# A conversion's first ScalarE step is moved from the end of one loop iteration to the middle of the next

## The chip, the cores and the metric

The kernel runs on one NeuronCore of a Trainium2 chip. The time is the device time of one execution in microseconds (us), and the number quoted is the median of several executions. The traces come from one further execution that the hardware profiler recorded. Matrix work is done by TensorE (PE in the rows, with its weight loads as PEld), elementwise work by VectorE (DVE), ScalarE (ACT) and GpSimd (POOL). All transfers are issued by SyncE (SP).

## The reference

Three layers follow each other. The first is a recurrent attention with a decaying state; the second a soft mixture of experts; the third a two-layer network with a squared ReLU. Inputs are float32.

```
for t in range(S):                                   # S = 768, 4 batches, 8 heads, D = 48
    cur = einsum('bhd,bhe->bhde', u * k_t, v_t)
    y_t = einsum('bhd,bhde->bhe', r_t, state + cur)
    state = w_t * state + einsum('bhd,bhe->bhde', k_t, v_t)
logits = x @ phi                                     # x: 3072 x 384, 32 slots
slot_in = softmax_over_tokens(logits).T @ x
slot_out[e] = relu(slot_in[e] @ w1[e]) @ w2[e]       # 8 experts, 384 -> 1024 -> 384
x = softmax_over_slots(logits) @ slot_out
h = relu(x @ w_in); out = (h * h) @ w_out            # 384 -> 2048 -> 384
```

The two weight matrices of the last layer arrive as 64-bit words. They are turned into float32 by integer arithmetic on the chip; this is what "conversion" means below.

## The kernel before

The attention runs in a loop of 33 iterations (line 531) with an order written out by hand: each engine executes its instructions in the order in which the Python code issues them. One unit is a pair of heads of one batch and half of the sequence (three chunks of 128 tokens). Iteration i works on several units at once. It starts the loads of unit i+4 and the v of unit i+2, scans the decay of unit i+2 (`scan0`, `scan1`, on DVE), transposes k of unit i+1 (`ktr`, on PE), and forms the state of unit i and the output of unit i-1. Batch b fills iterations 8b to 8b+7, and while the next batch runs, `slot` places its logits, softmax and slot sums into four places of the iterations.

The ring that passes through every iteration is this. `kvmm` (PE, tile psacc) multiplies the transposed k, `Kn`, with v. `state` (DVE, lines 252 and 254, tile S) adds the result to the decayed state. `tmul` (ACT, line 265, tile Tb) scales S, four small activations in even iterations and six in odd ones. `ycopy` (ACT, line 280) takes the output of the unit before from PSUM. `pend` (line 191) takes the decay products. `kcopy` (ACT, line 233) takes the transposed k from PSUM into `Kn`, and with that the next `kvmm` can begin. ACT's order in an iteration is tmul, ycopy, pend, kcopy, a small copy `dc` (line 174), and the copies of `slot`. DVE's order is scan0, state, a reciprocal, kprod, scan1, `amask` (line 218), two conversion steps, and the reductions of `slot`. GpSimd's is `diag0` (line 166, it needs a loaded rk), `diag5` (line 178), `rprod` (line 207, it needs scan1's F) and the last conversion step.

In 16 of the iterations a piece of w_in, 128 x 384 words, is converted. `LDW` is the list of iterations at whose end a piece j is loaded (5, 6, 7, 9, 10, 11, 13, 14, 15, 17, 18, 19, 21, 22, 23, 25). Line 465 issues this load into one of two buffers in turn. `wconv` (line 409) returns the four steps of a conversion:

```
q0: cc.q  = low words * 2^-29       ACT,  line 416
c2: cc.m  = high words << 3, masked DVE,  line 426
c3: cc.m |= sign and top bit        DVE,  line 430
c4: win   = cc.m + cc.q             POOL, line 434
```

There is one scratch tile `cc` in the loop. q0 of one conversion therefore has to wait for c4 of the conversion before it, which reads both halves of `cc`. c4 waits for its own q0 and c3. The load of piece j+2 has to wait for q0 and c3 of piece j, which read its buffer. In SP's queue the loads of the next iteration (lines 154 and 162) stand behind that load.

The list `cv` holds the steps of the conversion whose piece was loaded one iteration ago. It is filled at the end of iteration i; there q0 is issued, behind everything that iteration i gave to ACT and ahead of tmul of iteration i+1. The three other steps are issued in iteration i+1, behind `slot(i, 1)` (line 593).

Of the kernel before, what the change touches and what calls it, by code (L numbers as in the profile page):

```python
# [60 lines left out]
def rwkv_softmoe_relu2(ctx: ExitStack, tc: tile.TileContext, lt, lp, ub, vp, r, k, v, w, u, phi, phn, w1, w2, w_in, w_out, consts, xd, out):  # L61
# [72 lines left out]
    def mt(name):  # L134
        return psM.tile([128, 512], F32, tag="m", name=name)

    def warm(mt, n, src=cst[:, 0:256].bitcast(BF16)):
        ps = mt("warm")
        for _ in range(n):
            mm(ps, src[:, 0:128], src)  # L140
# [4 lines left out]
    def load(i, between=lambda: None):  # L145
        u_, hf = divmod(i, 2)
        b, p = divmod(u_, NP)
        t = {"i": i, "h": hf, "p": p, "b": b, "rk2": rk[i % NL], "w": lb[i % NW]}
        for o, c, n in ((t["w"], slice(LW, LN), NW), (t["rk2"], slice(0, LW), NL)):
            if i < n:  # L150
                nc.sync.dma_start(out=o, in_=lp[i, :, c])
            else:
                for h in range(2):
                    nc.sync.dma_start(out=o[64 * h:64 * h + D], in_=lt[b, 2 * p + h, hf, :, c])
            between()
            between = lambda: None
        t["r"], t["k"] = t["rk2"][:, 0:HT], t["rk2"][:, LK:LK + HT]
        return t

    def load_v(t):  # L160
        t["v"] = vt[t["i"] % NV]
        nc.sync.dma_start(out=t["v"][:, 0:2 * HC * D], in_=vp[t["b"], t["p"], t["h"]])
# [5 lines left out]
    def diag1(t, ps):  # L168
        for n in range(HC):
            mm(ps[:, HT + 2 * n:HT + 2 * n + 2], t["rk"][:, n * C:(n + 1) * C], uB[:, t["p"], 0:2])  # L170

    def diag2(t, ps):
        t["dc"] = P.tile([128, HC, 2], F32, tag="dc", name="dc", bufs=2)
        nc.scalar.copy(out=t["dc"], in_=chunks(ps[:, HT:HT + 2 * HC], 2))
# [7 lines left out]
    def scan0(t):  # L182
        q = t["Q"] = pq
        nc.vector.tensor_tensor_scan(
            out=q[:, 0:NZ][:, ::-1], data0=t["w"][:, ::-1], data1=b1[:, ::-1],
            initial=0.0, op0=ALU.mult, op1=ALU.add)
# [22 lines left out]
    def amm(t):  # L209
        ps = t["pA"] = psA.tile([128, 2, 512], F32, tag="A", name="psA")  # L210
        for n in range(HC):
            for h in range(2):
                q = slice(64 * h, 64 * h + 64)
                s = slice(n * C, (n + 1) * C)
                mm(ps[:, h, s], t["k"][q, s], t["r"][q, s])

    def amask(t):
        nc.vector.copy_predicated(  # L218
            out=t["A"], mask=mask.unsqueeze(1).unsqueeze(1).to_broadcast([128, HC, 2, C]),
            data=t["pA"][:, :, 0:HT].rearrange("p h (n c) -> p n h c", c=C))  # L220

    def ktr(t, t2=None):
        n = HC if t["h"] == 0 else HC - 1
        ps = t["pK"] = mt("psK")
        for j in range(n):
            tr(ps[:, j * C:(j + 1) * C], t["k"][:, j * C:(j + 1) * C])
        if t2:
            diag1(t2, ps)

    def kcopy(t, t2=None):  # L230
        n = HC if t["h"] == 0 else HC - 1
        kn = t["Kn"] = P.tile([128, HC, C], F32, tag="Kn", name="Kn", bufs=2)
        nc.scalar.copy(out=kn[:, 0:n, :], in_=chunks(t["pK"][:, 0:n * C]))  # L233
        if t2:
            diag2(t2, t["pK"])
# [4 lines left out]
    def kvmm(t):  # L240
        for n in range(HC if t["h"] == 0 else HC - 1):
            for h in range(2):
                q = slice(64 * h, 64 * h + 64)
                mm(kvs(t, n)[q], t["Kn"][:, n, q], t["v"][:, (2 * n + h) * D:(2 * n + h + 1) * D])

    def state(t, n):
        if n >= (HC if t["h"] == 0 else HC - 1):
            return
        s, kv = t["S"], kvs(t, n)
        o = t["Sn"][:, 0] if n == HC - 1 else s[:, n + 1]  # L250
        if n < (1 if t["h"] == 0 else 0):
            nc.vector.tensor_copy(out=o, in_=kv)  # L252
        else:
            nc.vector.scalar_tensor_tensor(
                out=o, in0=s[:, n], scalar=t["P"][:, n:n + 1], in1=kv, op0=ALU.mult, op1=ALU.add)

    def tmul(t, late=False):
        for n in range(1 if t["h"] == 0 else 0, HC):
            for h in range(2):
                q = slice(64 * h, 64 * h + 64)  # L260
                o, x, c = t["T"][q, n, 64 * h:64 * h + D], t["S"][q, n], t["P"][q, n:n + 1]
                if late:
                    nc.vector.tensor_scalar(out=o, in0=x, scalar1=c, scalar2=None, op0=ALU.mult)
                else:
                    nc.scalar.activation(out=o, in_=x, func=AF.Copy, scale=c)  # L265

    def ymm(t):
        ps = mt("psY")
        f = 1 if t["h"] == 0 else 0
        for n in range(HC):  # L270
            for h in range(2):
                mm(ps[64 * h:64 * h + 64, n * C:(n + 1) * C], t["v"][:, (2 * n + h) * D:(2 * n + h) * D + 64], t["A"][:, n, h, :],
                   start=(n == 0), stop=(n < f))
        for n in range(f, HC):
            s = slice(n * C, (n + 1) * C)
            mm(ps[:, s], t["T"][:, n, :], t["r"][:, s], start=False)
        t["pY"] = ps

    def ycopy(t):
        nc.scalar.copy(out=t["x"][:, t["h"] * HT:(t["h"] + 1) * HT], in_=t["pY"][:, 0:HT])  # L280
# [186 lines left out]
    def conv_win(j):  # L467
        return wconv(win.rearrange("p c f -> p (c f)")[:, DM * j:DM * j + DM], wst.pop(j), pa, DM, 2 * NZ)

    with tc.manual_schedule():  # L470
# [41 lines left out]
        xs, todo, cv = {}, {}, []  # L512
# [18 lines left out]
        for i in range(NH + 1):  # L531
            cur, nx1, nx2, prv = U.get(i), U.get(i + 1), U.get(i + 2), U.get(i - 1)
            if cur:
                cur["T"] = Tb[i % 2]
                cur["S"], cur["Sn"] = sb[i % 3], sb[(i + 1) % 3]
            if i + LA < NH:
                U[i + LA] = load(i + LA)
            nx3 = U.get(i + 3)
            if i + LV in U:
                load_v(U[i + LV])  # L540
            late = i >= NH - 2
            if cur:
                kvmm(cur)
            if late:
                if cur:
                    amm(cur)
                if nx1:
                    ktr(nx1)
                    kcopy(nx1)
            if prv:  # L550
                if prv["h"] == 0:
                    xs[i // 2] = X.tile([128, S], F32, tag="x", name="x", bufs=NX)
                prv["x"] = xs[(i - 1) // 2]
                ymm(prv)
            if cur and not late:
                amm(cur)
            if i == 0:
                warm(mt, WARMS[1], zero)
                ps = mt("psD")
                diag1(nx1, ps)  # L560
                diag2(nx1, ps)
            if nx1 and not late:
                ktr(nx1, nx2)
            if i == 0:
                warm(mt, WARMS[2], zero)
            if nx2:
                scan0(nx2)
            if cur:
                for n in range(HC):
                    state(cur, n)  # L570
                if late:
                    amask(cur)
                tmul(cur, late)
            if prv:
                ycopy(prv)
            if nx2:
                for f in (recip, kprod, pend, scan1):
                    f(nx2)
            if nx1 and not late:
                kcopy(nx1, nx2)  # L580
            slot(i, 0)
            if nx3 and i >= SW:
                diag0(nx3)
            if nx1:
                diag5(nx1)
            if cur and not late:
                amask(cur)
            if nx2:
                rprod(nx2)
            if nx3 and i < SW:  # L590
                diag0(nx3)
            slot(i, 1)
            while cv:
                cv.pop(0)()
            slot(i, 2)
            slot(i, 3)
            if cur:
                if i in LDW:
                    load_win(LDW.index(i))
                if i - 1 in LDW:  # L600
                    cv = conv_win(LDW.index(i - 1))
                    cv.pop(0)()
                while wq and len(wq) > NR1 * (NH - 2 - i) // (NH - 3):
                    put(wq.pop(0))
            if NH - NL < i <= NH - 3:
                put(NR1 + i - NH + NL - 1)
            for j in EARLY.get(i - NH, ()):
                put(NR + j)
            U.pop(i - 1, None)
# [606 lines left out]
```

## Time and profile before

| what | value |
|---|---|
| time, median of 3 runs | 444.8 us (444.07 to 449.06) |
| the profiled execution: its time / its span | 442.97 us / 441.1 us |
| busy in the whole span: PE, DVE, ACT, POOL | 95%, 80%, 65%, 30% |
| TensorE's granted clock, mean | 0.989 |
| chain that ended last, by engine | PE 82%, DMA 6%, ACT 5%, DVE 3%, POOL 2% |

The span runs from the first to the last instruction; the execution's own time is 1.87 us more. Conversions of w_in stand between 42.7 us and 150.6 us of the span. Shares of busy time are means over stages with different limits, so they are read by stage. The loop ends near 165 us; the experts' weights and w_out are loaded and used until about 208 us; the last layer's matrix products fill the rest.

### The profile page before, as it was taken

To read this page: it belongs to the slowest core of one execution; us is meant where nothing else is said; L and a number is where in the kernel's file an instruction comes from. 1 tells how busy PE (TensorE), PEld (TensorE's weight loads), DVE (VectorE), ACT (ScalarE), POOL (GpSimd) and SP (SyncE) were. 2 spreads that over 40 slices of the span, in tenths; PEclk is the share of its full clock that TensorE was granted. 3 is DMA by queue.
4 is the path that set the end of the run, shared out by engine and by line. 5 is a ranking of instruction groups with operands and counts; after the bars stand their busy time and mean duration, and the time that the engine had idled before them with its cause. 6 is when DMAs were issued, how large, how long until landed. Compare 5 with 4: busy or idle time off the path is not lost.

```text
span 441.1 us, 9152 instructions
## 1 busy us (share of the span) xinstructions
PE 417.6 (95%) x3218; PEld 327.6 (74%) x3220; DVE 353.7 (80%) x667; ACT 287.3 (65%) x707; POOL 134.0 (30%) x152
## 2 busy tenths in 40 slices
PE   7888999999899999997999999999999999999993
PEld 4677787778678876534788788888888888888882
DVE  7799999998999984466899668787887887887871
ACT  2466777677677735144887667777777777777661
POOL 3666676676676620014478000000000000000000
PEclk9699999999999999999999999999999999999998
DMA  8789898998979899899210442163244316316102
GB/s 250 215 235 270 232 270 224 257 276 226 290 221 257 230 373 333 313 405 395 62 25 0 137 151 89 55 215 107 91 158 136 116 68 204 106 53 216 37 0 79
DMA packets 47686, 81.38 MB, mean 184 GB/s; under 512 B 5616, under 2 KB 29776, under 8 KB 47632
## 3 DMA queue, kind: packets, MB, share of 16 engines
q1 hardware_dynamic: 47632, 80.72, 59.5%
q8 instruction: 27, 0.44, 0.4%
q14 instruction: 27, 0.22, 0.2%
HBM read 75.19 MB, written 4.72 MB: 181 GB/s over the span
## 4 chain that ended last, share of the span: by engine, by line
PE 82%; DMA 6%; ACT 5%; DVE 3%; POOL 2%; issue 1%; SPq 0%; ACTq 0%; POOLq 0%; DVEq 0%
PE pso L129 30%; PE psh L129 14%; PE psY L129 9%; PE psw L129 7%; PE psA L129 5%; PE psK L129 3%; PE psacc L129 3%; DMA wr<-in_w_out_dram 3%; DMA wr<-in_w_dram 3%; PE psx L132 2%; PE psK L132 2%; ACT Tb L265 2%; PE psLP L129 1%; PE psLN L129 1%; ACT Kn L233 1%
## 5 line engine op out<-in xcount | busy, mean ns | idle before, releaser
L772 ACT ACTIVATE a<-psh 128x512 f32<-128x512 f32 x96 | 57.5, 599 | 53.3 <-PE psh L129 52.9
L129 PE MATMUL pso<-gh,wr 128*128 128x512 f32 x288 | 84.2, 394 | 0.0
L780 DVE TENSOR_TENSOR a<-a 128x512 f32<-128x512 f32 x78 | 53.7, 689 | 30.5 <-ACT gh L779 30.4
L129 PEld LDWEIGHTS pso<-gh,wr 128*128 128x128 f32 x288 | 53.9, 188 | 12.0
L781 DVE TENSOR_TENSOR gl<-a,gh 128x512 fp32r<-128x512 f32 x78 | 54.0, 693 | 7.5
L265 ACT ACTIVATE Tb<-S,Pe 64x48 f32<-64x48 f32 x150 | 49.6, 331 | 15.0 <-DVE S L252 9.8
L779 ACT ACTIVATE gh<-a 128x512 fp32r<-128x512 f32 x78 | 49.3, 632 | 2.5
L129 PE MATMUL pso<-gl,wr 128*128 128x512 f32 x144 | 44.3, 389 | 0.0
L129 PE MATMUL psh<-cT,M_sb 128*128 128x512 f32 x96 | 38.2, 400 | 0.1
L166 POOL TENSOR_TENSOR rk<-rk 128x384 f32<-128x384 f32 x31 | 31.2, 1006 | 20.1 <-DMA rk<-in_lt_dram 11.1
L218 DVE COPY_PREDICATED A<-cst,psA 128x768 f32<-128x768 int32 x32 | 32.2, 1007 | 3.5 <-PE psA L129 3.3
L207 POOL TENSOR_TENSOR rk<-rk,F 128x384 f32<-128x384 f32 x31 | 29.1, 938 | 13.8 <-DVE F L198 11.9
L952 DVE TENSOR_REDUCE ext<-wh 128x1 f32<-128x384 f32 x64 | 32.2, 545 | 0.0
L178 POOL TENSOR_SCALAR_AFFINE_SELECT A<-dc 128x768 f32<-128x768 f32 x32 | 28.2, 880 | 11.2 <-issue 4.8
L129 PEld LDWEIGHTS pso<-gl,wr 128*128 128x128 f32 x144 | 27.0, 188 | 5.6
L129 PE MATMUL psA<-rk 64*128 64x128 f32 x384 | 30.1, 289 | 0.0
L129 PE MATMUL psw<-gh,wr 128*128 128x512 f32 x72 | 28.2, 392 | 0.0
L129 PE MATMUL psh<-gh,wr 128*128 128x512 f32 x72 | 28.2, 391 | 0.0
L129 PE MATMUL pso<-gh,rk 128*128 128x512 f32 x96 | 27.9, 396 | 0.0
L129 PE MATMUL psY<-A,v 128*64 128x128 f32 x384 | 27.7, 280 | 0.0
L129 PE MATMUL psY<-rk,Tb 128*128 128x128 f32 x160 | 26.9, 299 | 0.0
L129 PEld LDWEIGHTS psA<-rk 64*128 64x128 f32 x384 | 24.0, 187 | 3.8 <-issue 0.2
(196 smaller groups left out, 867.9 us busy)
## 6 DMA issues: line engine op xcount, KB each, us to landing
wr<-in_w_dram SPq DMA_DIRECT2D x44, 384.0 KB, 6.3
rk<-in_lt_dram SPq DMA_DIRECT2D x52, 144.0 KB, 4.9
wr<-in_w_in_dram SPq DMA_DIRECT2D x16, 384.0 KB, 5.3
wh<-in_w_in_dram SPq DMA_DIRECT2D x16, 384.0 KB, 3.5
wh<-in_w_out_dram SPq DMA_DIRECT2D x16, 384.0 KB, 3.3
v<-in_vp_dram SPq DMA_DIRECT2D x32, 144.0 KB, 4.7
wr<-in_w_out_dram SPq DMA_DIRECT2D x12, 384.0 KB, 7.9
out_dram<-ob SPq DMA_DIRECT2D x18, 256.0 KB, 2.2
```

The lines of the kernel that those rows point to most:

```text
L129: nc.tensor.matmul(out_, lhsT, rhs, start=start, stop=stop, skip_group_check=True)
L132: nc.tensor.transpose(out_, in_, ident[0:k, 0:k])
L166: eng.tensor_tensor(out=t["rk"], in0=t["r"], in1=t["k"], op=ALU.mult)
L178: nc.gpsimd.affine_select(out=a.rearrange("p n h c -> p (n h) c"), in_=t["dc"].rearrange("p n h -> p (n h)").unsqueeze(2).to_broadcast([12 ...
L207: eng.tensor_tensor(out=rv, in0=rv, in1=chunks(t["F"], CZ)[:, :, 0:C], op=ALU.mult)
L218: nc.vector.copy_predicated(out=t["A"], mask=mask.unsqueeze(1).unsqueeze(1).to_broadcast([128, HC, 2, C]), data=t["pA"][:, :, 0:HT].rearra ...
L265: nc.scalar.activation(out=o, in_=x, func=AF.Copy, scale=c)
L772: nc.scalar.activation(out=a, in_=ps, func=AF.Relu)
L779: return gh, gl, [lambda: nc.scalar.activation(out=gh, in_=a, func=AF.Square), lambda: nc.vector.tensor_tensor(out=a, in0=a, in1=a, op=ALU ...
L780: lambda: nc.vector.tensor_tensor(out=a, in0=a, in1=a, op=ALU.mult),
L781: lambda: nc.vector.tensor_tensor(out=gl, in0=a, in1=gh.bitcast(F32), op=ALU.subtract)]
L952: nc.vector.tensor_reduce(out=ext[:, i, j:j + 1], in_=wh[j][:, :, 1].bitcast(F32), axis=AX.X, op=o, apply_absolute_value=True)
```

## The change

The call that issued q0 right after the list of steps was made is removed. The list now still holds all four steps, and the loop at line 593 of the next iteration issues q0 there, directly ahead of c2, c3 and c4.

```
                 if i - 1 in LDW:
                     cv = conv_win(LDW.index(i - 1))
-                    cv.pop(0)()
                 while wq and len(wq) > NR1 * (NH - 2 - i) // (NH - 3):
                     put(wq.pop(0))
```

The line that now issues all four steps is unchanged: `while cv: cv.pop(0)()` (lines 593 and 594), between `slot(i, 1)` and `slot(i, 2)`. On ACT, q0 thus moves from ahead of tmul to behind dc and the copies of slots 0 and 1, and ahead of the copies of slots 2 and 3.

## Rows read from the trace of the kernel before

**Rows 1.** Busy time by stage: length, then each engine's busy time, clock, DMA share, GB/s.
```profile
42.00:155.00 113.00, 107.27 (x1286) 87.94 (x1286) 107.18 (x212) 81.02 (x256) 77.04 (x84) 1.00 0.93 250
68.00:98.00 30.00, 27.81 (x339) 22.68 (x340) 29.40 (x56) 21.27 (x68) 21.27 (x23) 1.00 0.99 258
177.00:208.00 31.00, 27.66 (x369) 14.14 (x365) 18.11 (x49) 11.28 (x27) 6.07 (x6) 1.00 0.99 372
```

**Rows 2.** ACT's waits from 42 to 155 us: total us, times, longest.
```profile
ACT cc L416 <- POOL win L434: 8.4, 7, 2.4
```

**Rows 3.** Timeline of iteration 13, all engines: start, us, instruction, [idle before <- releaser].
```profile
72.49 0.56 DVE L430 SCALAR_TENSOR_TENSOR cc<-wr,cc 128x384 uint32<-128x384 uint32 x1
...
73.19 1.00 POOL L434 TENSOR_TENSOR win<-cc 128x384 int32<-128x384 int32 x1 [0.95 <-DVE cc L430]
...
73.84 0.54 DVE L254 SCALAR_TENSOR_TENSOR S<-S,Pe,psacc 128x48 f32<-128x48 f32 x2
...
74.22 0.55 ACT L416 ACTIVATE cc<-wr 128x384 int32<-128x384 uint32 x1 [0.76 <-POOL win L434]
...
74.68 2.04 ACT L265 ACTIVATE Tb<-S,Pe 64x48 f32<-64x48 f32 x6
...
77.72 0.56 PE L129 MATMUL psacc<-v,Kn 128*64 128x48 f32 x12 [1.22 <-ACT Kn L233]
```

**Rows 4.** Timeline of PE and PEld: other idle stretches that ACT ended.
```profile
38.26 0.56 PE L129 MATMUL psacc<-v,Kn 128*64 128x48 f32 x12 [0.62 <-ACT Kn L233]
...
90.97 0.42 PEld L132 LDWEIGHTS psx<-cst,x 128*128 128x128 f32 x4 [0.29 <-ACT x L280]
...
97.10 0.86 PE L129 MATMUL psLN<-cst,LP 128*128 128x32 f32 x6 [0.40 <-ACT Pe L191]
...
118.60 0.56 PE L129 MATMUL psacc<-v,Kn 128*64 128x48 f32 x12 [1.66 <-ACT Kn L233]
...
131.80 0.42 PEld L132 LDWEIGHTS psx<-cst,x 128*128 128x128 f32 x4 [0.27 <-ACT x L280]
```

**Rows 5.** Timeline of ACT and DVE in iteration 21.
```profile
115.09 0.55 ACT L416 ACTIVATE cc<-wr 128x384 int32<-128x384 uint32 x1 [2.37 <-POOL win L434]
...
115.23 0.54 DVE L254 SCALAR_TENSOR_TENSOR S<-S,Pe,psacc 128x48 f32<-128x48 f32 x2
...
115.55 0.66 ACT L265 ACTIVATE Tb<-S,Pe 64x48 f32<-64x48 f32 x2
```

**Rows 6.** Groups by line, DVE, 37 to 155 us: busy, mean ns, idle before.
```profile
L284 DVE TENSOR_REDUCE mx<-cN 128x32 f32<-128x192 f32 x3 | 1.5, 499 | 0.7 <-ACT cN L360 0.7
L322 DVE SCALAR_TENSOR_TENSOR accT<-accT,fb,psacc 128x385 f32<-128x385 f32 x2 | 1.2, 614 | 0.4 <-PE psacc L129 0.4
L308 DVE TENSOR_TENSOR d<-cN,psmb 128x192 f32<-128x192 f32 x3 | 1.1, 354 | 1.4 <-ACT fb L304 1.1 <-PE psmb L129 0.3
```

**Rows 7.** Timeline of POOL and DVE, later in iteration 13.
```profile
76.72 1.01 POOL L207 TENSOR_TENSOR rk<-rk,F 128x384 f32<-128x384 f32 x1
...
77.00 1.15 DVE L430 SCALAR_TENSOR_TENSOR cc<-wr,cc 128x384 uint32<-128x384 uint32 x1
```

**Rows 8.** Groups by line and shape, 42 to 155 us: c3 and diag0.
```profile
L430 DVE SCALAR_TENSOR_TENSOR cc<-wr,cc 128x384 uint32<-128x384 uint32 x16 | 13.1, 821 | 0.6
...
L166 POOL TENSOR_TENSOR rk<-rk 128x384 f32<-128x384 f32 x22 | 22.2, 1009 | 15.8 <-DMA rk<-in_lt_dram 11.1 <-DVE rk L203 1.9 <-PE psA L129 1.1
```

**Rows 9.** Timeline of iteration 11, POOL and ACT.
```profile
67.73 1.00 POOL L434 TENSOR_TENSOR win<-cc 128x384 int32<-128x384 int32 x1 [1.21 <-DVE cc L430]
...
67.78 0.53 ACT L387 COPY xa<-psx 128x384 f32<-128x384 f32 x1
```

**Rows 10.** SP's waits, 42 to 155 us: total us, times, longest.
```profile
SPq L465 <- DVE cc L430: 16.7, 5, 4.0
```

**Rows 11.** Timeline of ACT in iteration 14.
```profile
79.22 1.37 ACT L265 ACTIVATE Tb<-S,Pe 64x48 f32<-64x48 f32 x4 [1.48 <-DVE S L252]
```

**Rows 12.** The chain that ended last, behind the loop.
```profile
179.87 7.22 DMA wr<-in_w_out_dram
```

More of the change, by code (lines that the diff above doesn't have):

```diff
@@ L601, in rwkv_softmoe_relu2 @@
                     cv = conv_win(LDW.index(i - 1))
-                    cv.pop(0)()
                 while wq and len(wq) > NR1 * (NH - 2 - i) // (NH - 3):
```

## Prediction

> **What bounds the kernel now.** I read four views in this order: busy time by stage, ACT's waits, the timeline around the longest of them, and the idle time of PE and DVE. In the stage of the conversions (42 to 155 us) PE is busy 107.27 of 113.00 us and DVE 107.18, so two engines are close to full there, and the DMA share is 0.93 [rows 1]. From 68 to 98 us DVE is busy 29.40 of 30.00 us: in that stretch it waits for almost nothing. ACT is busy 81.02 of 113.00 us, and its largest wait is the one that the change is about: q0 stands still for c4 of the conversion before it, 8.4 us in 7 of the 16 conversions, at most 2.4 us [rows 2].
>
> How such a wait reaches PE is seen in iteration 13 [rows 3]. c3 ends late at 73.05, GpSimd's c4 runs from 73.19 to 74.19, q0 stands 0.76 us for it and runs until 74.77; tmul begins at 74.68, though the first S was there at about 73.84 + 0.27 = 74.11. ACT comes to the k copy later, and PE idles 1.22 us before the next kvmm. In an early iteration without a conversion the same place idles 0.62 us [rows 4], so 0.60 us of it is the wait's doing.
>
> **The change part by part.** *Removed: q0's place ahead of tmul, and its wait.* At the new place c4 of the conversion before was issued a whole iteration earlier, so the 8.4 us of waiting go. What that is worth is read from PE's idle time, not from ACT's. It is 1.22 - 0.62 = 0.60 us at 77.72, 1.66 - 0.62 = 1.04 us at 118.60, 0.40 us at 97.10 (the sequence's last logits stand behind ycopy), 0.29 us at 90.97 and 0.27 us at 131.80 (transposes that stand behind ycopy) [rows 3, 4]. Sum 2.60 us. The other stalls of the seven end in slack: PE shows no idle time behind them.
>
> Two things take from this. At 118.60 the q0 that waited longest (2.37 us) ended at 115.64, but the first S came at 115.23 + 0.27 = 115.50, and tmul began at 115.55 [rows 5]. DVE was late, and without q0 tmul would begin 0.05 us earlier. The 1.04 us are DVE's, and 1.56 us are left. Then DVE itself: a gain on PE counts only where DVE waits for PE or ACT. In the whole stage its waits for results of ACT and PE in `slot` are 0.7, 0.4 and 1.4 us [rows 6], together 2.5 us, and those of the first batch lie ahead of the first stall that reached PE. The wait for fb (1.1 us of the 1.4) and two thirds of the 0.7 are within reach. PE can be ahead by 0.29 + 0.40 = 0.69 us when the first of them comes, in iteration 19, and by 0.27 us more and a little of the rest in batch 3. I take 1.1 us; the ends are 0 (DVE holds everything) and 2.60 us.
>
> *Moved: q0's own 0.55 us.* They are spent sixteen times, as before. At the new place they lie ahead of the copies of slots 2 and 3 and of tmul of the next iteration. Where no conversion follows, tmul waits for S anyhow, as the 1.48 us at 79.22 show [rows 11], and this covers the 0.55. Where another conversion follows, q0 has left the place ahead of that tmul, and ACT's sum up to there is the same. I take 0; the cover is DVE's lag, and if DVE ran ahead the price would be up to 0.55 us in each of the six iterations that end a run of conversions.
>
> *Added: c4 waits for a later q0.* In iteration 11 c4 began at 67.73, while ACT worked on dc and then copied xa from 67.78 to 68.31 [rows 9]. q0 can begin only then and ends at about 68.86, so c4 begins some 1.1 us later. By the same reading the delay is about 1.3 us in iterations 9 and 0.6 to 1.2 us in 19, 0.8 us in 8 and 0.4 us in 7, and nothing where slots 0 and 1 give ACT no copy. Behind c4 in GpSimd's queue stand diag0, diag5 and rprod. Most often diag0 waits for its load as it is: 11.1 us in the stage [rows 8], which hides the delay. Where it doesn't, rprod is later and meets c2 or c3.
>
> That meeting has a price in the trace. c3 takes 0.56 us alone [rows 3] and 1.15 us when rprod is under way [rows 7], so 0.59 us of a full DVE. Over the stage c3 sums to 13.1 us [rows 8]; 16 x 0.56 = 8.96, and (13.1 - 8.96) / 0.59 = 7 of 16 are hit now. The Trainium skill, SBUF — State Buffer, section "Who interferes with whom", says that a DVE instruction with two SBUF inputs contends with a GpSimd instruction that reads SBUF, and that the loser is blocked for the whole of the other. By that rule c3 in Rows 7 would end 0.56 us behind rprod, at 78.29; it ended at 78.15, so the trace nearly agrees, and the rule speaks against delaying anything on GpSimd.
>
> From the delays I expect a hit more in iterations 12 and 21 and a part of one in 8, and one fewer in 13 or 17, where rprod comes to stand behind c3. The ends are seven hits fewer (-4.1 us) and nine more (+5.3 us); the present 7 of 16 says that neither is near. I take one hit more, 0.5 us rounded.
>
> *Added in SP's queue.* The load of piece j+2 waits for the readers of its buffer. SP stands 16.7 us, five times, for c3 at that load [rows 10]. Now it waits for q0 too, and in iterations 7, 11 and 19 q0 ends after c3, by 0.4 to 1.3 us. The loads of the next iteration are behind it. The bounds are 0 and 0.4 + 1.3 + 1.3 = 3.0 us; I take 0, because these loads serve units two to four iterations ahead and the DMA share of 0.93 leaves room to catch up.
>
> **The sum.** -1.1 + 0 + 0.5 + 0 = -0.6 us. Behind the loop a stage follows that is limited by transfers (DMA share 0.99 from 177 to 208 us, and the chain passes through a transfer of 7.22 us there) [rows 1, 12]. Its transfers begin when PE has used the weights whose place they take, so it begins earlier with the loop, and I pass the 0.6 us on. The sum is made on an execution of 442.97 us (span 441.1 and 1.87 around it), 1.8 us below the median of 444.8 us. I subtract from the median: **444.2 us**.
>
> **The rivals.** *A: as summed*, 443.2 to 445.0 us, chance 0.48. *B: DVE does not hold PE back.* All 2.60 us that PE shows are won: 444.8 - 2.6 = 442.2 us. For it speaks that the chain that ended last is PE for 82% of the span; against it the 29.40 of 30.00 us of DVE, and Rows 5. Chance 0.17. *C: slower, by rprod meeting c3.* The place is GpSimd behind the delayed c4 and the delayed rk loads. It decides where an rprod that now ends ahead of c2 slips past c2's start. Five of the nine unhit c3 hit would cost 5 x 0.59 = 2.95 us, less the 1.1 us gained: 444.8 + 1.9 = 446.7 us. For it: with 7 of 16 hit already, rprod and c3 lie close together, and the SP delay pushes the same way. Against: diag0's long waits for DMA take up delays. Chance 0.23. *D: the transfers behind the loop end when they did*, because they are the limit and not their start; then 444.8 us, chance 0.12. That the change does not do what it says would be c2 waiting for q0 through the shared tile cc, which would put ACT's lateness on DVE; c2 and c3 write the other half of cc, so I leave it inside C.
>
> **How the numbers follow.** The range 441.4 to 447.2 us holds A, D, most of B with the spread of the executions below it, and C. A change over 1% is one of 4.4 us, about what a measurement of this kernel can tell from none. Faster by that needs B and several hits fewer: 0.05. Slower by it needs eight or nine more hits or the SP delay in full on top of C: 0.06. Within 1%: 0.89.
>
> **What would show it.** ACT's wait of q0 for win should be gone; PE's idle time before kvmm at the end of iteration 13 should be near 0.6 us, and that at the end of iteration 21 still above 1.5 us. GpSimd's c4 should show waits for ACT's cc in iterations 8, 9, 11 and 19. c3's sum tells of the hits: 13.7 us by A, 16 us by C. SP's load should wait for cc on ACT three times. I am wrong if DVE's busy share of the stage falls clearly below 95% while the time stays, or if the stage from 42 to 155 us changes by over 3 us either way.

## The result, and the profile after

The changed kernel takes 447.41 us (median of 12 executions, 443.85 to 452.0) against 444.1 us (12, 443.01 to 449.06) for the kernel before: a ratio of 1.0061, interval 1.0034 to 1.0088. The forecast was 444.2 us, a little faster; the kernel became slower, and the time lies 0.2 us above the range. Ratios here leave out executions over 1.5% above their kernel's fastest, which matters below, since the highest times drop out of the ratio and not out of the median.

The profiled execution took 450.09 us (span 448.3), 7.12 us more than that of before, at a granted clock of 0.966 (before 0.989). That is more than the 3.3 us between the medians: it is the third longest of its kernel's twelve executions, and the 442.97 us of before lie under all twelve of the other kernel. Where the 7.12 us lie is read from windows cut at the same event in both kernels, the start of an iteration's first kvmm. The stretches are iterations 7 to 13, 13 to 16, 16 to 21, 21 to 24, 24 to 31, everything behind, and the whole loop from 7. Columns: window, length, PE, PEld, DVE, ACT, POOL, granted clock, DMA share, GB/s. First the kernel before, from iteration 13 on:

```profile
72.84:86.54 13.70, 11.96 (x152) 9.91 (x148) 13.38 (x27) 9.76 (x31) 9.80 (x11) 1.00 1.07 271
86.54:113.28 26.74, 26.03 (x310) 21.30 (x306) 25.07 (x50) 19.20 (x61) 18.21 (x20) 1.00 0.91 250
113.28:127.38 14.10, 11.93 (x153) 9.88 (x149) 13.76 (x29) 9.30 (x30) 9.75 (x11) 1.00 1.00 269
127.38:161.34 33.96, 33.05 (x399) 27.21 (x395) 31.83 (x63) 22.19 (x71) 21.30 (x23) 1.00 0.88 257
161.34:441.14 279.80, 268.94 (x1519) 207.72 (x1519) 206.90 (x377) 183.42 (x377) 30.56 (x32) 0.99 0.42 146
...
42.67:161.34 118.67, 112.83 (x1352) 92.63 (x1352) 112.11 (x223) 83.39 (x264) 79.31 (x85) 1.00 0.93 256
```

The same stretches of the changed kernel, and three short windows inside them:

```profile
43.09:73.21 30.12, 29.84 (x356) 24.34 (x356) 28.64 (x57) 22.97 (x71) 20.16 (x22) 1.00 0.88 238
73.21:91.16 17.95, 15.55 (x153) 12.46 (x149) 15.83 (x29) 9.96 (x32) 10.36 (x12) 0.78 0.93 234
91.16:118.04 26.88, 26.64 (x309) 22.14 (x305) 23.26 (x49) 19.63 (x61) 17.38 (x19) 0.96 0.79 228
118.04:133.74 15.70, 13.57 (x153) 11.12 (x149) 14.43 (x28) 8.91 (x31) 10.18 (x11) 0.89 1.04 263
133.74:167.24 33.50, 32.63 (x398) 27.15 (x394) 31.42 (x64) 23.02 (x72) 20.25 (x22) 1.00 0.90 257
167.24:448.26 281.02, 270.38 (x1520) 209.17 (x1519) 207.03 (x377) 183.61 (x377) 30.61 (x32) 0.99 0.42 146
...
43.09:167.24 124.15, 118.23 (x1351) 97.22 (x1351) 113.58 (x223) 84.49 (x264) 78.33 (x85) 0.95 0.89 244
...
83.30:93.50 10.20, 9.90 (x70) 7.57 (x71) 7.75 (x17) 4.56 (x15) 5.98 (x8) 0.50 0.75 199
127.60:131.00 3.40, 3.26 (x24) 2.62 (x24) 3.33 (x7) 2.06 (x7) 0.78 (x2) 0.51 1.05 275
209.60:213.00 3.40, 3.08 (x15) 3.08 (x16) 1.20 (x4) 1.79 (x6) 0.68 (x1) 0.50 1.04 403
```

The loop is 124.15 - 118.67 = 5.48 us longer. Two stretches hold it: 13 to 16 (+4.25) and 21 to 24 (+1.60). The instructions are the same to one or two, yet PE is busy 15.55 us in place of 11.96: the granted clock is 0.50, the level of 1.2 GHz, from 83.3 to 93.5 us and from 127.6 to 131.0 us, where it was 1.00 (2.4 GHz) in before. Such a stretch at 0.50 is called a fall below. The first fall reaches 2.3 us into the stretch 16 to 21. The stretch 24 to 31, with no fall, is 0.46 us shorter. The part behind the loop is 1.22 us longer, with a third fall, and the loop begins 0.42 us later.

What came just ahead of the falls stands in the timeline of the changed kernel, iterations 11 to 15 and 21 to 22, all engines (start, us, engine, instruction, [idle before <- releaser]):

```profile
68.71 0.58 ACT L416 ACTIVATE cc<-wr 128x384 int32<-128x384 uint32 x1
69.31 0.35 SPq L465 DMA_DIRECT2D wr<-in_w_in_dram  x1
69.37 1.00 POOL L434 TENSOR_TENSOR win<-cc 128x384 int32<-128x384 int32 x1 [2.35 <-ACT cc L416]
72.11 0.42 SPq L162 DMA_DIRECT2D v<-in_vp_dram  x1
77.78 0.56 PE L129 MATMUL psacc<-v,Kn 128*64 128x48 f32 x12 [0.90 <-DMA v<-in_vp_dram]
82.62 0.44 PE L129 MATMUL psacc<-v,Kn 128*64 128x48 f32 x8 [0.95 <-ACT Kn L233]
83.60 0.70 PE L129 MATMUL psY<-A,v 128*64 128x128 f32 x4 [0.55 <-DVE A L218]
...
118.05 0.67 ACT L265 ACTIVATE Tb<-S,Pe 64x48 f32<-64x48 f32 x2
120.26 1.37 ACT L265 ACTIVATE Tb<-S,Pe 64x48 f32<-64x48 f32 x4 [1.55 <-DVE S L254]
122.64 0.56 PE L129 MATMUL psacc<-v,Kn 128*64 128x48 f32 x12 [0.93 <-ACT Kn L233]
127.64 0.57 PE L129 MATMUL psacc<-v,Kn 128*64 128x48 f32 x6 [1.10 <-ACT Kn L233]
```

In iteration 11, q0 ends at 69.29, and only then does SP issue the load at line 465 (69.31). v of unit 14 is queued behind it and goes at 72.11. In the kernel before the same two loads stand at these times (timeline of SP):

```profile
67.65 0.35 SPq L465 DMA_DIRECT2D wr<-in_w_in_dram  x1
...
70.44 0.42 SPq L162 DMA_DIRECT2D v<-in_vp_dram  x1
```

Counted from the start of the loop windows (42.67 and 43.09), the first load is 1.24 us later and v 1.25 us later. Its transfer is also slower (DMA issues in a short window around v's: KB each, us from issue to landing), first before, then changed:

```profile
v<-in_vp_dram SPq DMA_DIRECT2D x1, 144.0 KB, 4.6
```

```profile
v<-in_vp_dram SPq DMA_DIRECT2D x1, 144.0 KB, 5.5
```

So v is late at 77.78, and PE idles 0.90 us for a DMA where before it idled 1.22 us for ACT [rows 3]: a wait has taken the place of the one removed. Two more waits follow, of 0.95 and 0.55 us, and the first fall begins in the second of these. The other begins at the wait that ends at 127.64; no v is late there (that of unit 23 landed 2.32 us ahead of its kvmm), but c3 at 123.22 took 1.15 us, and tmul then waited 2.13 us for DVE's S.

The waits of SP and POOL in the changed kernel (42 to 160 us: total us, times, longest):

```profile
POOL win L434 <- ACT cc L416: 17.1, 10, 2.9
...
SPq L465 <- DVE cc L430: 14.9, 6, 3.9
SPq L465 <- ACT d L310: 3.2, 2, 1.6
SPq L465 <- ACT cc L416: 2.0, 2, 1.6
```

ACT's wait for win [rows 2] is gone from ACT's list. Beside SP's wait for c3 [rows 10] there are now waits for ACT. Those put down to `d` are waits for q0 too: in iteration 11 the load goes 0.02 us behind q0's end, with `d` just begun.

### The profile page after: what moved, and what is told of

Read it like the earlier page. It is cut to its first block, busy times and chain, and to the rows that moved or that the text cites. A ratio compares the mean times of both kernels' runs of the same rounds, so it can differ in the third digit from the quotient of the medians.

```text
span 448.3 us, 9160 instructions
## 1 busy us (share of the span) xinstructions
PE 425.7 (95%) x3220; PEld 335.0 (75%) x3220; DVE 355.3 (79%) x667; ACT 288.5 (64%) x707; POOL 133.2 (30%) x152
## 4 chain that ended last, share of the span: by engine, by line
PE 79%; DMA 11%; DVE 3%; ACT 3%; issue 2%; POOL 1%; SPq 1%; DVEq 0%; ACTq 0%; POOLq 0%
PE pso L129 30%; PE psh L129 13%; PE psY L129 8%; PE psw L129 7%; PE psA L129 5%; DMA wr<-in_w_dram 3%; DMA wr<-in_w_out_dram 3%; PE psK L129 3%; PE psacc L129 3%; PE psK L132 2%; PE psx L132 2%; PE psLP L129 1%; DMA rk<-in_lt_dram 1%; PE psLN L129 1%; ACT Kn L233 1%
## 5 line engine op out<-in xcount | busy, mean ns | idle before, releaser
L129 PE MATMUL psA<-rk 64*128 64x128 f32 x384 | 31.5, 299 | 0.0
L129 PE MATMUL psY<-A,v 128*64 128x128 f32 x384 | 29.8, 295 | 0.6 <-DVE A L218 0.5
L129 PEld LDWEIGHTS psA<-rk 64*128 64x128 f32 x384 | 25.1, 195 | 3.9 <-issue 0.4
```

Of the source, the lines that this page charges most:

```text
L129: nc.tensor.matmul(out_, lhsT, rhs, start=start, stop=stop, skip_group_check=True)
```

## The experiments

The rival theories after the first trace: **K**, the time is lost to the falls of the clock, not to longer work; **Q**, it starts in SP's queue, where the load waits for the later q0; **V** and **D**, finer: what sets a fall off is the late v, or DVE's lag that PE meets afterwards.

**The two kernels again.** No edit. One execution's trace can't tell a habit from an accident.

> The changed kernel once more, for a second trace. Theory K (clock): the extra time is spent where TensorE's granted clock falls to 0.50 inside the loop, which the first trace shows twice (10.2 us from 83.3 us, 3.4 us from 127.6 us); a second trace shows such stretches again between iterations 13 and 24, of other lengths, and where it has fewer of them its loop is shorter by about half their length; outside them the loop is 1 to 2 us shorter than before. Rival Q (queues): the extra time is in waits behind the later q0 (the w_in load in SP's queue, c4 in GpSimd's), the same in every trace, 2 to 3 us with the clock at 1.00. Ratio to before 1.003 to 1.009 by both.

> The changed kernel, for a third trace. K: one or two falls between iterations 13 and 24, loop 120 to 125 us; Q: 120 to 121 us whatever the clock does.

> The changed kernel on the same chip as the two others, for the comparison: ratio 1.003 to 1.009, clock 0.978 to 0.985, and the loop in its trace 120 to 125 us with one or two falls in iterations 13 to 24.

> The kernel before, for a second trace. K: it has PE waits of 1.2 to 1.7 us behind iterations 13 and 21 as well, so its granted clock can fall there too in some executions; in this one either none (loop from iteration 7 to 31 about 118.7 us) or one fall behind iteration 13 or 21, with 2 us more for one of 3.4 us and 5 us more for one of 10.2 us. Q: no fall, 118.7 us.

Measured: after_again 447.66 us against 443.94 (ratio 1.0034, interval 0.9983 to 1.0085); after_fourth 445.31 against 443.76 (1.0019, 0.9981 to 1.0057); single executions, after_third 445.3 and before_again 441.16. Only the first comparison's interval keeps clear of 1; the medians of the repeats are 3.72 and 1.55 us above before's. The median granted clock of the executions was 0.980 and 0.9835 for the changed kernel, 0.988 and 0.985 for before beside them. The trace of after_fourth has no fall in the loop (the stretches 13 to 16, 16 to 21, 21 to 24, and the loop):

```profile
70.66:85.19 14.53, 12.13 (x153) 9.99 (x149) 14.18 (x28) 9.47 (x32) 9.56 (x11) 1.00 1.05 275
85.19:111.02 25.83, 25.59 (x309) 21.25 (x305) 24.94 (x50) 19.90 (x62) 18.24 (x20) 1.00 0.86 247
111.02:125.24 14.22, 12.15 (x153) 10.00 (x149) 13.98 (x29) 8.90 (x31) 9.05 (x10) 1.00 1.03 277
...
40.53:158.76 118.23, 112.37 (x1352) 92.74 (x1352) 113.92 (x223) 84.31 (x264) 78.99 (x85) 1.00 0.94 259
```

With the clock up, the changed loop is 118.67 - 118.23 = 0.44 us shorter than before's. So Q as it was put for these runs, 2 to 3 us of waits at a clock of 1.00, fails; what is left of it is that the queue brings the falls about. The kernel before falls too, in some executions, as before_again shows in its stretch 13 to 16:

```profile
70.69:85.86 15.17, 13.43 (x153) 11.21 (x149) 13.48 (x27) 9.76 (x31) 10.14 (x11) 0.89 1.01 259
```

So falls are not new. Two traces of before and four of the changed kernel are too few to count them by; over the executions, 14 of the changed kernel's 37 had a clock below 0.980, and 22 of the 120 of before beside the runs. Prices from the changed kernel's stretches with and without: a fall of 3.4 us cost 15.23 - 14.53 = 0.70 us in after_again's stretch 13 to 16, 16.05 - 14.22 = 1.83 us in its 21 to 24, and 15.70 - 14.22 = 1.48 us in 21 to 24 of the first trace; 6.8 us cost 17.52 - 14.22 = 3.30 us (after_third). The one of 10.2 us lies in two stretches, 13 to 16 and 16 to 21, and cost 17.95 + 26.88 - 14.53 - 25.83 = 4.47 us. The Trainium skill, TensorE: Matmul & The Clock Gate, section "Terms", puts the penalty at the time below full rate times (1 - K/N), where K of N clock pulses are passed; at half rate that gives an estimate of 1.7, 3.4 and 5.1 us. The trace agrees for 6.8 us, lies on either side of it for 3.4 us, and is below it for 10.2 us. Over the executions of after_again, those with a clock of 0.988 or more have a median of 443.05 us (4 of 12), the others 447.98; of before beside them 442.75 (19 of 35) and 445.33. The clock of an execution is a mean over all of it, and counts falls that the change can't have caused: before, with none in the loop, has 0.989, for a fall of 6.8 us ahead of the loop, and before_again 0.994 with the one in its loop.

**Work for PE in its waits.** Three matmuls on constants, results unused, at the first of the four places (slot 0) of iterations 13, 14, 21, 22, 29 and 30; in before_warm without the last two. after_warm_elsewhere is the control: the same matmuls in iterations 10, 11, 18 and 19, at a place where PE doesn't wait.

```
+        steps["w3"] = lambda: warm(mt, 3)        # before_warm, control: ... if b < 2 else None
+             5: ("w3", "", "", ""), 6: ("w3", "", "", "")       # control: at 2 and 3, third place
```

> The changed kernel with three dummy matmuls (128x512, bf16, some 0.2 us each) in slot 0 of the iterations 8b+13 and 8b+14, where PE waits for the k copy or for v. K: PE has work in the waits, the granted clock stays 1.00 in the loop, and the time falls to before's or 1 us below it (ratio 0.996 to 1.001). Q: the waits stay and PE's fill only adds; ratio 1.005 to 1.010.

> The kernel before with the three dummy matmuls in iterations 13, 14, 21 and 22. K: it has the same PE waits behind iteration 13 (1.22 us) and 21 (1.66 us), so some of its executions lose clock there too; the median falls by 0 to 2 us (0.995 to 1.000) and the slow tail of its executions shortens. Q: PE's work in the waits is worth nothing or costs up to 0.6 us in each; 1.000 to 1.003.

> The changed kernel with the same three dummy matmuls in iterations 10, 11, 18 and 19, where PE has work anyway. It is the control of after_warm: the same extra matmuls, but not in the waits. K: the waits of iterations 13 to 15 and 21 to 23 stay empty, the clock falls as in the changed kernel, and the dummies cost up to 0.64 us each: ratio 1.004 to 1.012. If dummies help wherever they stand, 0.998 to 1.002.

Measured: after_warm 443.45 us against 443.94 (1.0004, 0.9974 to 1.0034), median clock 0.9895; the plain changed kernel, on the same chip, 447.66 at 0.980. before_warm 442.89 against 444.35 (0.9974, 0.994 to 1.0007), clock 0.9935. The control 446.00 against 444.89 (1.0037, 1.0002 to 1.0073). The trace of after_warm, stretches 13 to 16 and 21 to 24, and then two of its timeline rows:

```profile
71.63:86.13 14.50, 13.40 (x159) 10.27 (x155) 14.15 (x28) 9.48 (x32) 9.75 (x11) 1.00 1.06 273
...
112.05:126.57 14.52, 13.49 (x159) 10.29 (x155) 14.28 (x29) 8.90 (x31) 9.13 (x10) 1.00 1.05 267
```

```profile
75.16 0.81 PE L129 MATMUL warm<-cst 128*128 128x512 bf16 x3
...
81.00 0.44 PE L129 MATMUL psacc<-v,Kn 128*64 128x48 f32 x8 [0.55 <-ACT Kn L233]
```

The stretches take 14.50 and 14.52 us, where after_fourth without a fall has 14.53 and 14.22; nothing in them became shorter, work was added, and the median is 4.2 us below that of the kernel without it. That speaks for K, but not as strongly as the medians say: the ratio goes from 1.0034 to 1.0004 alone, and the two intervals overlap. The control was to keep the falls, and didn't: its traced loop has none, its clock is 0.989 over the executions, and v of unit 14 lands 1.61 us ahead. So it isn't shown that the matmuls have to stand in the waits; they may also help by holding PE back while the loads arrive. Its time is above before's because it pays for its matmuls where PE has no time for them, 31.57 us in iterations 7 to 13 against 30.12.

**SP's queue freed.** Three ways: a third buffer for the loads (after_3raw; before_3raw is the same on the kernel before), v's load ahead of the piece's load in the queue (after_v_first), and q0 at the start of the iteration, ahead of slot 0 (after_q0_early; after_q0_early_3raw has both).

```
-        wst[j] = fresh(NR1 - 1 - j % 2, U32)...
+        wst[j] = fresh(NR1 - 1 - j % 3, U32)...            # after_3raw, before_3raw
```

```
+            if i - 1 in LDW:                               # after_v_first: behind the load of v;
+                load_win(LDW.index(i - 1))                 # the calls at the iteration's end go
+            if i - 2 in LDW:
+                cv = conv_win(LDW.index(i - 2))
```

```
+            if cv:                                         # after_q0_early: ahead of slot(i, 0)
+                cv.pop(0)()
```

> The changed kernel with three raw buffers for w_in in place of two, so that SP's load of a piece waits for a q0 and c3 that are an iteration or more past. Q: SP's waits at that load (14.9 + 3.2 + 2.0 + 1.2 us in the first trace) go, v of unit 14 lands before its product needs it, and the time comes 2 to 3 us down (ratio 0.999 to 1.002). K: PE's wait for v (0.90 us) goes, but the waits for the k copy and the mask stay, and with them most falls of the clock; ratio 1.002 to 1.007.

> The kernel before with three raw buffers for w_in, q0 at its old place. Q: the 16.7 us that SP stands at line 465 go, rk and v land earlier, fewer c2 and c3 meet a GpSimd instruction (their sum of 20.0 us falls to about 17 us), and the time falls by 1 to 3 us (ratio 0.993 to 0.998). K: the loop's DVE-full stretches stay, the clock stays as it is in the kernel before, and the time stays (0.998 to 1.002).

> The changed kernel, in which SP issues the load of a w_in piece behind the next iteration's loads of rk and v in place of ahead of them (two buffers, as before); q0 stays where the change put it. Theory V: the falls of the clock start with the late v (it lands 0.14 to 1.2 us ahead of its product in iteration 14 of the changed kernel, 2.7 to 3.2 us ahead before). Then they become as rare as in the kernel before: mean granted clock of the median execution 0.987 to 0.990, ratio 0.996 to 1.001. Theory D: they start with DVE's lag in iterations 14, 15, 22 and 23, which stays: clock 0.978 to 0.983, ratio 1.002 to 1.007.

> The changed kernel with q0 directly behind kcopy, ahead of the copies of slots 0 and 1, so that c4 and SP's load wait for it no longer than for c3, but the transposes' copies come 0.55 us later in eight iterations. Q: the waits for q0 go, the time is back at before's or 1 us less (0.996 to 1.001). K: PE's waits in iterations 14, 15, 22 and 23 are DVE's and stay; the granted clock still falls in some executions; 1.000 to 1.005.

> after_q0_early with three raw buffers, so neither SP nor c4 waits for q0 longer than for c3. V: as after_3raw, 0.996 to 1.000, clock 0.987 to 0.990. D: as after_q0_early, 1.000 to 1.004, clock 0.977 to 0.982.

| kernel | median, us | before beside it | ratio, interval | median clock |
|---|---|---|---|---|
| after_3raw | 442.75 | 443.94 | 0.9986, 0.9948 to 1.0024 | 0.988 |
| before_3raw | 445.08 | 444.35 | 0.9986, 0.9954 to 1.0018 | 0.985 |
| after_v_first | 443.18 | 443.76 | 0.9978, 0.9942 to 1.0013 | 0.989 |
| after_q0_early | 446.31 | 444.35 | 1.0014, 0.9972 to 1.0057 | 0.9785 |
| after_q0_early_3raw | 442.78 | 443.76 | 0.996, 0.9923 to 0.9997 | 0.988 |

The ways that free v put the changed kernel at or below the time of before: after_3raw is 4.9 us below the plain changed kernel beside it, after_v_first 2.1 us and after_q0_early_3raw 2.5 us below after_fourth beside them. The third buffer gives the kernel before nothing (c2 and c3 stay at 20.2 us there, where about 17 were expected), so it is not a gain of its own: it takes away what the change added. In after_3raw v of unit 14 landed 5.35 us ahead of its kvmm, in after_v_first 2.13 us, in before 2.73 us, in the changed kernel 0.14 us (in the repeats: 3.19 for before, 0.14, 1.16 and 0.68 for the changed one). This is Q. It does not single out v, though: in after_3raw and after_v_first c3 meets no GpSimd instruction any more. Its 16 sum to 8.9 us, or 0.56 each, and c2 and c3 together to 17.3 (after_3raw) and 18.0 us (after_v_first), where the four traces of the changed kernel have 20.7 to 24.1. The loads of rk, which GpSimd waits for, stand in the same queue; that they are the reason is likely and not shown. after_q0_early is the useful miss: its q0 is earlier, yet six of its loads still go 0.03 us behind q0's end, v has 1.45 us, and seven of its twelve executions, at clocks of 0.973 to 0.979, took 446.3 to 448.5 us, the five at 0.992 or 0.993 took 442.2 to 442.7. With the third buffer on top, two of twelve are that long (446.41 and 447.31 us).

V against D stays undecided for a single fall. The trace of after_3raw, where v is early, has none in 13 to 16 and one in 21 to 24:

```profile
70.73:84.34 13.61, 12.14 (x153) 9.99 (x149) 13.26 (x28) 9.57 (x32) 10.06 (x11) 1.00 0.92 258
...
110.17:125.62 15.45, 13.70 (x152) 11.30 (x148) 13.77 (x29) 8.92 (x31) 10.04 (x11) 0.89 0.98 262
```

So a fall needs no late v. after_v_first has one too, of 3.4 us in 13 to 16, and before_3raw one of 10.2 us in 21 to 24, as long as any in a loop here, with v 4.50 us ahead:

```profile
112.86:131.32 18.46, 16.28 (x153) 13.66 (x149) 14.42 (x30) 9.29 (x30) 10.26 (x12) 0.72 0.91 265
```

And after_fourth, with v 0.68 us ahead of its kvmm, has none. A late v adds to PE's waits; it is not the only thing that sets a fall off.

**Versions that take the gain without the loss.** q_two_buffers leaves q0 where the kernel before has it and writes the low half into two buffers in turn, so that q0 need not wait for c4. The other two add a third load buffer and the matmuls in the waits (batches 0 and 1).

```
+        return wconv(..., qt=(pairs["cc"], pairs["lb"])[j % 2][:, NZ:NZ + DM])     # q_two_buffers
```

> The kernel before, q0 at its old place, but q kept in two buffers in turn (a free half of another tile), so that q0 no longer waits for c4 of the conversion before, and c4 and SP's load do not come to wait for a later q0. It is the removed wait by itself. My forecast's sum for that part: 1.1 us shorter, at most 2.6 us (ratio 0.994 to 0.998). K: shorter by 1 to 2 us only if the clock stays up; if PE's waits in iterations 14, 15, 22 and 23 draw it down as in the changed kernel, 1.002 to 1.006. Q: 0.994 to 0.998.

> The changed kernel with three raw buffers and with the three dummy matmuls in iterations 13, 14, 21 and 22. K and Q together: no fall of the clock in the loop, SP's waits gone; the loop from iteration 7 to 31 takes 116 to 117 us (118.7 before), the time is 2 to 3 us below before (ratio 0.993 to 0.997) and spreads less. Q alone: the dummies add nothing to after_3raw, 0.998 to 1.000.

> All that helped in one kernel: q0 at its old place, q in two buffers, three raw buffers, dummy matmuls in iterations 13, 14, 21 and 22. K: no fall of the clock in the loop, no wait of q0 for c4, no wait of SP: loop 116 to 117 us, ratio 0.992 to 0.996. Q: as q_two_buffers, 0.998 to 1.003.

Measured: q_two_buffers 443.92 us against 443.94 (1.0023, 0.9984 to 1.0063), clock 0.9855; after_3raw_warm 442.76 against 444.35 (0.9952, 0.9913 to 0.9992), clock 0.9925; q_two_3raw_warm 440.14 against 444.89 (0.9907, 0.9872 to 0.9942; 10 executions), clock 0.993. The last beats both kernels. In q_two_buffers the traced loop, without a fall, is 1.38 us shorter than before's 118.67, and the median is the same:

```profile
71.19:84.47 13.28, 12.13 (x152) 9.99 (x149) 12.97 (x27) 9.86 (x31) 9.85 (x11) 1.00 1.07 278
...
41.01:158.30 117.29, 112.48 (x1351) 92.75 (x1351) 112.76 (x223) 84.44 (x264) 78.92 (x85) 1.00 0.93 253
```

A shorter loop at a lower clock (0.9855 against 0.988 beside it) is no faster kernel: taking the wait away is worth something only together with a clock that stays up. This kernel also prices the parts of the change, from one trace each of a loop without a fall: the removed wait by itself is 1.38 us, and what the later q0 adds is 118.23 - 117.29 = 0.94 us.

## Why the prediction was wrong

**The step that failed** is "Added in SP's queue", with "I take 0, because these loads serve units two to four iterations ahead". The delay itself was worked out rightly, 1.3 us in iteration 11 (measured 1.24), and in after_fourth, without a fall, three loads go right behind q0, in iterations 7, 11 and 19, as forecast. In the first trace six do, and q0 ends 6.2 us after c3 in them together, against the bound of 3.0. The cover was given in iterations and not read in us: v of unit 14 landed 2.73 us ahead of its kvmm in before and 0.14 us ahead in the changed kernel. Of the 2.6 us, 1.25 are the queue, 1.0 the slower transfer, and 0.36 come from kvmm itself, which starts earlier, counted from the loop's start (77.78 - 43.09 = 34.69 against 77.72 - 42.67 = 35.05). "the DMA share of 0.93 leaves room to catch up" took the mean over the stage; from 68 to 98 us the share is 0.99 [rows 1], which leaves next to none. At a clock of 1.00 the step costs little, as the 0.94 us above say; it is paid in the falls that come behind PE's waits. What shows it is that the changed kernel with its loads freed is back at or below the time of before, and its median clock at 0.988 or 0.989.

**A term was missing**: the granted clock. Rows 1 show 1.00 for every stage, and the sum took PE's durations as fixed. The falls cost 4.47 + 1.48 = 5.95 us in the profiled loop, and the loop is 5.48 us longer: they are the whole of its loss. At a clock of 1.00 the sum was nearly right, 0.44 us shorter (after_fourth) against 0.6, and its parts fair: 1.38 us gained for 1.1, 0.94 added for 0.5. The range had no place for falls; its upper end of 447.2 stands on C's hits.

**The removed wait.** Right in direction: the wait is gone, and 1.1 us was a fair price. The reading of iteration 21 [rows 5] was wrong. The first two tmul activations ran at 118.05, before that unit's S was there (the four behind them wait 1.55 us for it), so they need only an earlier state and q0 did hold them. PE's idle time at the end of this iteration became 0.93 us, not "still above 1.5 us". The gain was repaid one iteration later at DVE, as 1.10 us at 127.64, so DVE's holding PE back, the reason for taking 1.1 of 2.60 us, stands.

**The idle time in iteration 13**, forecast near 0.6 us, is 0.90 us, and its releaser is a DMA; in after_again it is 1.28 us, with v again 0.14 us ahead. In after_third and after_fourth v is in time, and the 0.57 us are the forecast's. There the gain is repaid one kvmm later, where before idles 0.52 us; the rows of after_fourth:

```profile
74.89 0.56 PE L129 MATMUL psacc<-v,Kn 128*64 128x48 f32 x12 [0.57 <-ACT Kn L233]
...
80.06 0.44 PE L129 MATMUL psacc<-v,Kn 128*64 128x48 f32 x8 [1.28 <-ACT Kn L233]
```

**rprod, c2 and c3.** c4 waits for q0 as forecast, more often than in the four iterations named (10 times, 17.1 us). The groups of c3 and c2 in the changed kernel (42 to 155 us: busy, mean ns, idle before):

```profile
L430 DVE SCALAR_TENSOR_TENSOR cc<-wr,cc 128x384 uint32<-128x384 uint32 x16 | 11.8, 740 | 0.6
L426 DVE TENSOR_SCALAR cc<-wr 128x384 uint32<-128x384 uint32 x16 | 9.2, 577 | 0.0
```

and of c2 in the kernel before:

```profile
L426 DVE TENSOR_SCALAR cc<-wr 128x384 uint32<-128x384 uint32 x16 | 6.9, 428 | 0.0
```

c3 [rows 8] is 1.3 us shorter and c2 2.3 us longer, together 1.0 us more, where 0.5 was forecast from c3 alone. That c3 is shorter is an accident of this pair of traces: in the repeats it is at 13.0, 12.7 and 13.5 us, and at 10.1 in before_again. c2 and c3 together are at 20.7 to 24.1 us in four traces of the changed kernel, 20.0 and 18.6 in two of before. The Trainium skill, SBUF — State Buffer, section "Who interferes with whom", names tensor_scalar too among the DVE operations that can contend with GpSimd; the trace agrees, c2's mean going from 428 to 577 ns, and the forecast had priced c3 alone. Rival C names nearly the measured time, 446.7 us, but its row fails, c3 at 16 us, in all four traces. Its mechanism is there, partly in c2, but at a clock of 1.00 it costs the loop little: after_fourth has c2 and c3 at 22.7 us and the shorter loop. Whether it helps to set off the falls is open. Without the rows C would have been taken for confirmed.

**Behind the loop** the 0.6 us should have been passed on. That part is 281.0 to 281.2 us in all four traces of the changed kernel and 279.8 and 279.9 in the two of before, with a fall of 3.4 us some 43 us behind the loop's end. PE waits 1.7 to 2.8 us for ACT at this place in every trace of every kernel. The fall follows in ten of the seventeen, before_3raw and after_3raw among them, and there the part takes 280.9 to 281.7 us; without it 279.8 to 280.9. So these 1.2 us go with the fall and not with SP's queue; why it came in all four traces of the changed kernel is open. Open also is which of PE's waits sets off a fall in a given execution, and why three of the first twelve executions of the changed kernel took 443.85, 447.57 and 447.85 us at clocks of 0.988 to 0.994. Nor is it shown that the clock accounts for all of the loss over the executions: in those of after_again at lower clocks the median is still 2.65 us above that of before at lower clocks, but their clock is lower too, 0.9775 against 0.9845.

## What to carry to other kernels

When a step moves later, list every queue that waits for it, and for each the first transfer behind the waiting one with its margin from arrival to use; here a delay of 1.25 us used up a cover of 2.7, because the transfer slowed down too and its user came earlier. When a wait of a nearly full PE is exchanged for another of the same length, compare the granted clock over many executions before counting it as even. A change that shortens the work can lose to the clock, so an edit of this kind is worth trying together with something for PE to do in its waits.

## What the runs showed of the hardware

PE's granted clock fell from 1.00 to 0.50 in a loop in which PE was busy 112.37 of 118.23 us when no fall came, behind waits of 0.3 to 1.9 us each, and stayed there for 3.4, 6.8 or 10.2 us. The changed kernel had 0 to 2 such falls in its loop in one execution and the next; two of them, 13.6 us together, made the loop 5.9 us longer (124.15 against 118.23). With three unused matmuls of 0.81 us together in PE's waits, at six places of the loop, the median clock was 0.9895 and not 0.980. c2 and c3, 0.34 and 0.56 us when nothing was in their way, took up to 0.94 and 1.15 us in the changed kernel's first trace, beside a GpSimd instruction.
